# Float64 weights narrowed by a rounded integer low part from ScalarE and one integer add on GpSimd

## The chip, the cores and the metric

One core of one Trainium2 chip runs the whole program. The metric is the device time of one execution in microseconds (us); what is compared is the median over several executions. The engines are named as in the profile: PE is TensorE, DVE is VectorE, ACT is ScalarE, POOL is GpSimd and SP is SyncE, whose queue issues all the DMAs of this kernel.

## The reference

Attention with packed queries, then a gated feed-forward block, then a second feed-forward block, over 4608 tokens of width 512. The weight matrices arrive as float64 (the division by a square root promotes them), everything else as float32.

```
q, k, v: (8, 8, 576, 64)   p: (8, 8, 32, 64)   float32
p_packed = softmax_attention(p, k, v)
out      = softmax_attention(q, p_packed, p_packed)      -> x (4608, 512)
xn  = x / rms(x) * rms_g
g   = xn @ w_gate ;  val = xn @ w_val                    (512 x 1536, float64)
y   = (silu(g) * val) @ w_out                            (1536 x 512, float64)
h   = y @ w_in ;  a = max(h, 0) + alpha * min(h, 0)      (512 x 2048, float64)
out = a @ w_out2                                         (2048 x 512, float64)
```

## The kernel before

The tokens are cut into nine chunks of 512. Each chunk of the first feed-forward block runs 12 steps `f`: a matmul group into `ps_g` (gate), one into `ps_v` (value), `s = silu(g)` on ACT (L736), `s = s * v` on DVE (L742), a split of `s` into a high part `hh` (ACT, L68) and a low part `hl` (DVE, L71), and a matmul group into `ps_y`. Every product is three matmuls of high and low parts (L80 to L82). After all nine chunks, the second block runs over `y` read back from DRAM. Attention for the next chunk is cut into small steps (`k_steps`, `q_steps`) that are placed between the matmul groups at 34 places per chunk, by the function `attn`.

Before chunk 0 there is a prologue: it loads p, k, v and q, runs the attention of the first 512 tokens on banks of their own, with a few idle matmuls (`warmup`) between, and starts to narrow the weights. Each engine runs its instructions in the order in which the Python code emits them; nothing reorders them.

The narrowing is what the change touches. A weight unit is 128 x 512 float64 values, loaded as pairs of 32-bit words into a tile `w` (tag w64; `lo` and `hi` are its even and odd words, so each of them has a stride of 8 bytes). Units come in jobs of six: four of gate and value weights (`gv`, four DMAs each, L167) and two of `w_out` (`o`, one DMA each, L172); six jobs make the 36 units of the first block. `narrow` makes a float32 tile (`gv_raw` or `w_raw`) of a unit:

- L186, DVE: shift and mask of `hi` into the float32 tile.
- L191, ACT, on the units with `pool` set: `lo` scaled to a float.
- L193, DVE: sign and exponent bits of `hi` merged in. The tile is then the truncated float32.
- L197, DVE: the exponent alone, written over `hi`.
- L201, POOL (with `pool`): `lo` times the exponent, in place; or L204, DVE (without): scale and product in one instruction.
- L208, POOL: the tile plus that product, in float.

`narrow` is a generator: every `yield` ends a step. `conv(n)` runs `n` steps, two units alternating; `conv_to(m)` runs steps until `m` units are done. A unit of pool form has three steps, one of the other form four. The prologue asks for 30 steps; each of the 34 places of chunk 0 asks for three, and each `f` of chunk 0 forces with `conv_to` that the units it needs are done. A narrowed `gv` unit is also written to DRAM (L219, SP) so that later chunks can read it back (L562). The 32 units of the second block are narrowed by `conv_late` at the places that the table `LATE` selects in chunks 1 and on, and written to DRAM (L227).

The wide tiles come from a ring: nine slots for units 0 to 17, four (`NST`) for units 18 to 35. A load into a slot waits until the last instruction that reads the slot's old unit, which is the add on POOL, has ended. The loads, the writes of L219 and the loads of k, v and q (L122, L125, L137) all stand in one SP queue, in order: one that waits holds up all behind it.

Of the kernel before, what the change touches and what calls it, by code (L numbers as in the profile page):

```python
# [8 lines left out]
F32 = mybir.dt.float32  # L9
F32R = mybir.dt.float32r  # L10
I32 = mybir.dt.int32
U32 = mybir.dt.uint32
ACTF = mybir.ActivationFunctionType
ALU = mybir.AluOpType
# [4 lines left out]
def attention_moe_moe2_kernel(ctx, tc, q, k, v, p, w_gate, w_val, w_out, rms_g, w_in2, w_out2, alpha, out):  # L19
    nc = tc.nc  # L20
# [18 lines left out]
    scale = 1.0 / float(D) ** 0.5  # L39
# [2 lines left out]
    NST = 4  # L42
    SLOTS = dict(enumerate(["k"] * 10 + ["kk"] + ["k"] * 6 + ["a"]))
    SLOTS.update({20: "a", 21: "ba", 23: "a", 24: "a", 25: "a", 26: "b", 27: "b", 28: "a", 29: "b", 30: "b", 31: "b", 32: "b"})
    LATE = [int(i % 3 != 2) for i in range(34)]

    const = ctx.enter_context(tc.tile_pool(name="const", bufs=1))
    wa = ctx.enter_context(tc.tile_pool(name="wa", bufs=NF))
# [13 lines left out]
    def bank(tag):  # L62
        if tag in ("g", "v", "at", "wg"):
            return ps.tile([128, 512], F32, tag="m", name="ps_" + tag, bufs=4)
        return ps.tile([128, 512], F32, tag=tag, name="ps_" + tag)
# [18 lines left out]
    with tc.manual_schedule():  # L84
# [65 lines left out]
        raw, staged = {}, {}  # L150
# [8 lines left out]
        def load_wide(u, pool, bufs):  # L159
            t = pool.tile([128, 4, 128, 2], I32, tag="w64", name="w64", bufs=bufs)  # L160
            if u[0] == "gv":
                j, dc = divmod(u[1], 4)
                tf = t.rearrange("p c x w -> p (c x w)")
                for i, w in enumerate((w_gate, w_val)):
                    src = w.bitcast(I32).rearrange("(g c d) x -> c g d x", g=G, c=HG)[dc]
                    for g in range(G):
                        nc.sync.dma_start(  # L167
                            out=tf[g * D:(g + 1) * D, i * 512:(i + 1) * 512],
                            in_=src[g, :, j * 512:(j + 1) * 512],
                        )  # L170
            else:
                nc.sync.dma_start(out=t.rearrange("p c x w -> p c (x w)"), in_=src_of(u).bitcast(I32))  # L172
            return t

        def new_gv():
            return one.tile([128, 4, 128], F32, tag="gv", name="gv_raw", bufs=8)
# [2 lines left out]
            half = n * 2 // NU1  # L179
            staged[n] = load_wide(units[n], (sg, one)[half], (NSG, NST)[half])  # L180

        def narrow(t, w, pool):
            lo, hi = t[:, :, :, 0], t[:, :, :, 1]
            wi = w.bitcast(I32)
            r = lo.bitcast(F32)
            nc.vector.tensor_scalar(  # L186
                out=wi, in0=hi, scalar1=3, scalar2=0x3FFFFFF8,
                op0=ALU.logical_shift_left, op1=ALU.bitwise_and,
            )
            if pool:  # L190
                nc.scalar.activation(out=r, in_=lo.bitcast(U32), func=ACTF.Copy, scale=2.0 ** -52)  # L191
            yield
            nc.vector.scalar_tensor_tensor(  # L193
                out=wi, in0=hi, scalar=-0x40000000, in1=wi, op0=ALU.bitwise_and, op1=ALU.bitwise_or
            )
            yield
            nc.vector.tensor_scalar(  # L197
                out=hi, in0=wi, scalar1=-0x800000, scalar2=None, op0=ALU.bitwise_and
            )
            if pool:  # L200
                nc.gpsimd.tensor_tensor(out=r, in0=r, in1=hi.bitcast(F32), op=ALU.mult)  # L201
            else:
                yield
                nc.vector.scalar_tensor_tensor(  # L204
                    out=r, in0=lo.bitcast(U32), scalar=2.0 ** -52, in1=hi.bitcast(F32),
                    op0=ALU.mult, op1=ALU.mult,
                )
            nc.gpsimd.tensor_tensor(out=w, in0=w, in1=r, op=ALU.add)  # L208

        def conv_unit(n, pool):  # L210
            if n == NU1 // 2:
                sg_ctx.close()
                late_pools["wg2"] = ctx.enter_context(tc.tile_pool(name="wg2", bufs=NWG - NWG1, reuse_waits="tile"))
            u = units[n]
            w = new_gv() if u[0] == "gv" else wa.tile([128, 4, 128], F32, tag="w", name="w_raw")
            yield from narrow(staged.pop(n), w, pool)
            raw[u] = w
            if u[0] == "gv":
                nc.sync.dma_start(out=gv_dram[u[1]], in_=w.rearrange("p c x -> p (c x)"))  # L219
            yield  # L220

        def conv_late():
            ahead = [load_wide(u, one, NST) for u in units2[:2]]
            for i, u in enumerate(units2):
                w = one.tile([128, 4, 128], F32, tag="w32", name="w32", bufs=2)
                yield from narrow(ahead.pop(0), w, i % 2)
                nc.sync.dma_start(out=w_dram[i], in_=w)  # L227
                if i + 2 < len(units2):
                    ahead.append(load_wide(units2[i + 2], one, NST))
                yield  # L230
# [3 lines left out]
        def loads_to(n):  # L234
            while n_load[0] < min(n, NU1):
                m = n_load[0]
                old = m - (NSG, NST)[m * 2 // NU1]
                if old >= n_conv[0] and old >= 0 and old * 2 // NU1 == m * 2 // NU1:
                    break
                load_unit(m)  # L240
                n_load[0] += 1

        def conv_all():
            while n_conv[0] < NU1:
                n = n_conv[0]
                loads_to(NU1)
                while n // 6 > n_job[0] + 1:
                    yield
                live = [conv_unit(n, 1), conv_unit(n + 1, 1 if n % 3 else 0)]
                while live:  # L250
                    for g_ in list(live):
                        if next(g_, live) is live:
                            live.remove(g_)
                            n_conv[0] += 1
                            loads_to(NU1)
                        else:
                            yield
            while True:
                yield

        convs = conv_all()
        late = conv_late()

        def conv(n):
            for _ in range(n):
                next(convs, None)
# [337 lines left out]
        def warmup(n):  # L604
            for _ in range(n):
                nc.tensor.matmul(warm_bank[:, 0:128], lhsT=ident, rhs=ident, start=True, stop=True)

        def run(g_, n=1):
            for _ in range(n):
                next(g_, None)  # L610
# [13 lines left out]
        for n in range(14):  # L624
            run(gk)
            if n == 9:
                run(qa)
            if n in (6, 8, 10, 11, 12):
                conv(2)
        nc.sync.dma_start(out=alpha_sb, in_=alpha.rearrange("(f p) -> p f", p=128))  # L630
        for n, (g_, k_) in enumerate([(qa, 1), (qb, 1), (qa, 1), (qa, 1), (qb, 1), (qa, 2), (qb, 1), (qa, 1), (qb, 1), (qb, 3)]):
            conv(2)
            run(g_, k_)
            warmup(3)
        conv_to(4)
# [45 lines left out]
        for c in range(NCH):  # L681
# [10 lines left out]
            def attn():  # L692
                for g_ in SLOTS.get(slot[0], ""):
                    if g_ in gens:
                        run(gens[g_])
                slot[0] += 1
                if c == 0:
                    conv(3)
                elif not last and LATE[slot[0] - 1]:
                    next(late, None)  # L700

# [20 lines left out]
            for f in range(NF):  # L722
# [12 lines left out]
                s = ring.tile([128, T], F32, tag="s", name="s")  # L735
                nc.scalar.activation(out=s, in_=tg, func=ACTF.Silu)  # L736
                attn()
                if last and f == NF - 1:
                    both(("i2", 0))
                    both(("i2", 1))  # L740
                tv = blk_in(f, 256, "v")
                nc.vector.tensor_tensor(out=s, in0=s, in1=tv, op=ALU.mult)  # L742
                hs[f] = hsplit(s)
                attn()
                if f % 2:
                    if f < NF - 1:
# [5 lines left out]
                if f and f < NF - 1:  # L752
                    attn()
# [49 lines left out]
        for k_, (c, f) in enumerate(steps):  # L803
            if f == 0:
                ycur = ynext
            t = bank("g")
            wh, wl = in_s.pop(("i2", f))
            for d in range(KD):
# [3 lines left out]
                out=s, in0=t, scalar1=0.0, scalar2=alpha_sb[:, f:f + 1], op0=ALU.min, op1=ALU.mult  # L812
# [47 lines left out]
```

## Time and profile before

| | us |
|---|---|
| median of three runs | 1780.98 (1780.61 to 1782.32) |
| profiled execution, its own time | 1781.89 |
| its span | 1780.1 |
| busy in the span: PE, DVE, ACT, POOL | 1716.0, 1067.9, 776.4, 164.9 |
| prologue, up to the transposes of `x` for chunk 0 | 66.25 |
| chunk 0, from there to those for chunk 1 | 136.44 |
| chunk 1, likewise | 107.81 |

Stretches are cut where PE begins the transposes (L545) that make the `xh` and `xl` of a chunk: at 66.25, 202.69 and 310.50 us. A row of the waits view says which engine and line sat idle, for whose instruction, and for how long in total. In a row of the group view, the mean of one instruction counts from its start to its end, so an instruction that is held after it has started shows a long duration, not idle time. The granted clock of PE (PEclk) is a share of its full speed.

### The profile page before, as it was taken

The page shows a single profiled execution, that of the slowest core. Times are in us where ns is not written, and L with a number is a line of the kernel's source. Part 1 is how long each engine was busy: PE and PEld are TensorE (multiplying, and loading weights), DVE is VectorE, ACT ScalarE, POOL GpSimd, SP SyncE. Part 2 cuts the span into 40 slices and gives each one's busy share as a digit, 9 for nine tenths or more (in the row PEclk, how much of TensorE's full clock was granted, in tenths as well). Part 3 has the DMA queues.
Part 4 walks back from the last instruction along what each step waited for, and adds up shares of the span by engine and source line. Part 5 has one row for each costly group of instructions (what it writes and reads, how often), then busy time and mean ns, then how long its engine had stood idle before and what let it go on. Part 6 is the DMA issues. An engine that isn't in the chain of part 4 may idle for free.

```text
span 1780.1 us, 25459 instructions
## 1 busy us (share of the span) xinstructions
PE 1716.0 (96%) x9932; PEld 1395.2 (78%) x9932; DVE 1067.9 (60%) x1774; ACT 776.4 (44%) x1360; POOL 164.9 (9%) x142
## 2 busy tenths in 40 slices
PE   5778999999999999999999999999999999999999
PEld 4545778888888888888888888888888888888887
DVE  3888555655656665444344666666666666666665
ACT  2444455555555555554444333333333333333332
POOL 2565111011111111000000000000000000000000
PEclk7988999999999999999999999999999999999999
DMA  7857354555646463322142201010101010100000
GB/s 187 231 167 220 120 166 124 168 143 165 186 148 170 158 178 103 108 83 87 45 149 83 77 1 48 1 48 1 48 1 47 1 47 1 48 1 24 1 24 24
DMA packets 159064, 161.58 MB, mean 91 GB/s; under 512 B 88288, under 2 KB 102624, under 8 KB 158944
## 3 DMA queue, kind: packets, MB, share of 16 engines
q1 hardware_dynamic: 158944, 159.96, 29.7%
q8 instruction: 78, 1.28, 0.3%
q14 instruction: 42, 0.34, 0.1%
HBM read 126.36 MB, written 33.55 MB: 90 GB/s over the span
## 4 chain that ended last, share of the span: by engine, by line
PE 88%; DVE 4%; ACT 3%; DMA 2%; SPq 2%; issue 1%; POOL 0%; DVEq 0%; ACTq 0%
PE ps_y L80 13%; PE ps_y L82 12%; PE ps_y L81 12%; PE ps_g L82 11%; PE ps_g L80 11%; PE ps_g L81 11%; PE ps_v L80 3%; PE ps_v L81 3%; PE ps_v L82 3%; PE ps_wg L573 2%; PE ps_at L502 2%; PE ps_at L468 1%; SPq L167 1%; ACT L736 1%; PE ps_at L313 1%
## 5 line engine op out<-in xcount | busy, mean ns | idle before, releaser
L68 ACT ACTIVATE hh<-s2m 128x512 fp32r<-128x512 f32 x144 | 91.0, 632 | 493.7 <-DVE s2m L814 493.7
L71 DVE TENSOR_TENSOR in_l<-w_raw,in_h 128x512 fp32r<-128x512 f32 x306 | 211.0, 708 | 33.1 <-ACT in_h L68 28.8
L68 ACT ACTIVATE in_h<-w_raw 128x512 fp32r<-128x512 f32 x306 | 191.7, 627 | 80.9 <-PE ps_y L81 71.2
L81 PE MATMUL ps_g<-yl,in_h 128*128 128x512 f32 x576 | 226.6, 393 | 0.0
L80 PE MATMUL ps_g<-yh,in_h 128*128 128x512 f32 x576 | 226.3, 393 | 0.0
L82 PE MATMUL ps_y<-in_h,hl 128*128 128x512 f32 x576 | 226.0, 392 | 0.0
L82 PE MATMUL ps_g<-yh,in_l 128*128 128x512 f32 x576 | 225.8, 392 | 0.0
L80 PE MATMUL ps_y<-in_h,hh 128*128 128x512 f32 x576 | 225.2, 391 | 0.0
L81 PE MATMUL ps_y<-in_l,hh 128*128 128x512 f32 x576 | 223.9, 389 | 0.0
L811 DVE TENSOR_SCALAR s2m<-ps_g,alpha_sb 128x512 f32<-128x512 f32 x144 | 108.1, 750 | 162.9 <-PE ps_g L82 162.9
L80 PE MATMUL ps_y<-hh,in_h 128*128 128x512 f32 x432 | 180.4, 418 | 0.0
L81 PE MATMUL ps_y<-hl,in_h 128*128 128x512 f32 x432 | 169.4, 392 | 0.2 <-DVE hl L71 0.2
L82 PE MATMUL ps_y<-hh,in_l 128*128 128x512 f32 x432 | 169.5, 392 | 0.0
L71 DVE TENSOR_TENSOR hl<-s2m,hh 128x512 fp32r<-128x512 f32 x144 | 99.8, 693 | 109.3 <-ACT hh L68 109.3
L742 DVE TENSOR_TENSOR s<-s,ps_v 128x512 f32<-128x512 f32 x108 | 74.2, 687 | 128.2 <-PE ps_v L82 116.6
L68 ACT ACTIVATE hh<-s 128x512 fp32r<-128x512 f32 x108 | 68.2, 631 | 145.4 <-DVE s L742 144.9
L80 PE MATMUL ps_g<-xh,wgh 128*128 128x512 f32 (+7 forms) x384 | 126.5, 329 | 2.2 <-ACT xh L68 1.0
L80 PE MATMUL ps_v<-xh,wgh 128*128 128x512 f32 (+7 forms) x384 | 128.2, 334 | 0.0
L82 PEld LDWEIGHTS ps_g<-yh,in_l 128*128 128x128 f32 x576 | 108.1, 188 | 24.9
L81 PEld LDWEIGHTS ps_g<-yl,in_h 128*128 128x128 f32 x576 | 108.0, 188 | 25.0
L82 PE MATMUL ps_g<-xh,wgl 128*128 128x512 f32 (+7 forms) x384 | 122.9, 321 | 4.9 <-DVE wgl L71 4.8
L80 PEld LDWEIGHTS ps_g<-yh,in_h 128*128 128x128 f32 x576 | 108.1, 188 | 25.0
(151 smaller groups left out, 3095.7 us busy)
## 6 DMA issues: line engine op xcount, KB each, us to landing
gv_raw<-gv_dram SPq DMA_DIRECT2D x168, 256.0 KB, 4.2
w<-in_moe_w_out_dram SPq DMA_DIRECT2D x28, 512.0 KB, 4.0
kt<-in_k_dram SPq DMA_DIRECT2D x64, 144.0 KB, 3.5
vt<-in_v_dram SPq DMA_DIRECT2D x16, 576.0 KB, 5.6
y_dram<-stg SPq DMA_DIRECT2D x18, 512.0 KB, 2.7
y_raw<-y_dram SPq DMA_DIRECT2D x9, 1024.0 KB, 6.5
qt<-in_q_dram SPq DMA_DIRECT2D x64, 128.0 KB, 3.4
w<-in_moe_w_in_dram SPq DMA_DIRECT2D x16, 512.0 KB, 4.0
```

Of the source, the lines that this page charges most:

```text
L68: nc.scalar.activation(out=hi, in_=src, func=ACTF.Copy)
L71: nc.vector.tensor_tensor(out=lo, in0=src, in1=hi.bitcast(F32), op=ALU.subtract)
L80: nc.tensor.matmul(out=o, lhsT=lh, rhs=rh, start=first, stop=False)
L81: nc.tensor.matmul(out=o, lhsT=lh, rhs=rl, start=False, stop=False)
L82: nc.tensor.matmul(out=o, lhsT=ll, rhs=rh, start=False, stop=last)
L167: nc.sync.dma_start(out=tf[g * D:(g + 1) * D, i * 512:(i + 1) * 512], in_=src[g, :, j * 512:(j + 1) * 512],)
L313: nc.tensor.matmul(out=t[c * 64:(c + 1) * 64, 0:w], lhsT=pT[:, 2 * g + c, :], rhs=kT[g][:, c * S + hf * w:c * S + (hf + 1) * w], start=Tru ...
L468: nc.tensor.matmul(out=tv[off:off + n, k_, j], lhsT=qT[i][:, j, off:off + n], rhs=ppB[b % 2][:, j, :], start=True, stop=True,)
L502: nc.tensor.matmul(out=t[off:off + n, g * 256:(g + 1) * 256], lhsT=A2T[0][:, k_, g, off:off + n], rhs=ppbd[b % 2][:, :, g, :], start=True, ...
L573: nc.tensor.matmul(out=ts[g][h * NP:(h + 1) * NP, :], lhsT=ppG[b][g * D:(g + 1) * D, h, :], rhs=us[h][g * D:(g + 1) * D, :], start=True, s ...
L742: nc.vector.tensor_tensor(out=s, in0=s, in1=tv, op=ALU.mult)
L811: nc.vector.tensor_scalar(out=s, in0=t, scalar1=0.0, scalar2=alpha_sb[:, f:f + 1], op0=ALU.min, op1=ALU.mult)
```

## The change

L197, L201 and L204 go. ACT now runs on every unit, with another scale, and writes `lo` back as a rounded 32-bit integer in units of the float32's last place. POOL adds that integer to the bits of the truncated float32 in one integer add, where it had a float product and a float add. A unit has two steps instead of three or four, so the counts of steps change with it: in the prologue 2 of the 14 places of the first loop call `conv(2)` instead of 5, the second loop calls `conv(1)` instead of `conv(2)` (14 steps, seven units, instead of 30 steps), chunk 0 asks for two steps per place, and `LATE` selects every third place instead of two of three.

```diff
--- before.py
+++ after.py
@@ -42,7 +42,7 @@
     NST = 4
     SLOTS = dict(enumerate(["k"] * 10 + ["kk"] + ["k"] * 6 + ["a"]))
     SLOTS.update({20: "a", 21: "ba", 23: "a", 24: "a", 25: "a", 26: "b", 27: "b", 28: "a", 29: "b", 30: "b", 31: "b", 32: "b"})
-    LATE = [int(i % 3 != 2) for i in range(34)]
+    LATE = [int(i % 3 == 0) for i in range(34)]
 
     const = ctx.enter_context(tc.tile_pool(name="const", bufs=1))
     wa = ctx.enter_context(tc.tile_pool(name="wa", bufs=NF))
@@ -179,41 +179,27 @@
             half = n * 2 // NU1
             staged[n] = load_wide(units[n], (sg, one)[half], (NSG, NST)[half])
 
-        def narrow(t, w, pool):
+        def narrow(t, w):
             lo, hi = t[:, :, :, 0], t[:, :, :, 1]
             wi = w.bitcast(I32)
-            r = lo.bitcast(F32)
             nc.vector.tensor_scalar(
                 out=wi, in0=hi, scalar1=3, scalar2=0x3FFFFFF8,
                 op0=ALU.logical_shift_left, op1=ALU.bitwise_and,
             )
-            if pool:
-                nc.scalar.activation(out=r, in_=lo.bitcast(U32), func=ACTF.Copy, scale=2.0 ** -52)
+            nc.scalar.activation(out=lo, in_=lo.bitcast(U32), func=ACTF.Copy, scale=2.0 ** -29)
             yield
             nc.vector.scalar_tensor_tensor(
                 out=wi, in0=hi, scalar=-0x40000000, in1=wi, op0=ALU.bitwise_and, op1=ALU.bitwise_or
             )
-            yield
-            nc.vector.tensor_scalar(
-                out=hi, in0=wi, scalar1=-0x800000, scalar2=None, op0=ALU.bitwise_and
-            )
-            if pool:
-                nc.gpsimd.tensor_tensor(out=r, in0=r, in1=hi.bitcast(F32), op=ALU.mult)
-            else:
-                yield
-                nc.vector.scalar_tensor_tensor(
-                    out=r, in0=lo.bitcast(U32), scalar=2.0 ** -52, in1=hi.bitcast(F32),
-                    op0=ALU.mult, op1=ALU.mult,
-                )
-            nc.gpsimd.tensor_tensor(out=w, in0=w, in1=r, op=ALU.add)
-
-        def conv_unit(n, pool):
+            nc.gpsimd.tensor_tensor(out=wi, in0=wi, in1=lo, op=ALU.add)
+
+        def conv_unit(n):
             if n == NU1 // 2:
                 sg_ctx.close()
                 late_pools["wg2"] = ctx.enter_context(tc.tile_pool(name="wg2", bufs=NWG - NWG1, reuse_waits="tile"))
             u = units[n]
             w = new_gv() if u[0] == "gv" else wa.tile([128, 4, 128], F32, tag="w", name="w_raw")
-            yield from narrow(staged.pop(n), w, pool)
+            yield from narrow(staged.pop(n), w)
             raw[u] = w
             if u[0] == "gv":
                 nc.sync.dma_start(out=gv_dram[u[1]], in_=w.rearrange("p c x -> p (c x)"))
@@ -223,7 +209,7 @@
             ahead = [load_wide(u, one, NST) for u in units2[:2]]
             for i, u in enumerate(units2):
                 w = one.tile([128, 4, 128], F32, tag="w32", name="w32", bufs=2)
-                yield from narrow(ahead.pop(0), w, i % 2)
+                yield from narrow(ahead.pop(0), w)
                 nc.sync.dma_start(out=w_dram[i], in_=w)
                 if i + 2 < len(units2):
                     ahead.append(load_wide(units2[i + 2], one, NST))
@@ -246,7 +232,7 @@
                 loads_to(NU1)
                 while n // 6 > n_job[0] + 1:
                     yield
-                live = [conv_unit(n, 1), conv_unit(n + 1, 1 if n % 3 else 0)]
+                live = [conv_unit(n), conv_unit(n + 1)]
                 while live:
                     for g_ in list(live):
                         if next(g_, live) is live:
@@ -625,11 +611,11 @@
             run(gk)
             if n == 9:
                 run(qa)
-            if n in (6, 8, 10, 11, 12):
+            if n in (6, 10):
                 conv(2)
         nc.sync.dma_start(out=alpha_sb, in_=alpha.rearrange("(f p) -> p f", p=128))
         for n, (g_, k_) in enumerate([(qa, 1), (qb, 1), (qa, 1), (qa, 1), (qb, 1), (qa, 2), (qb, 1), (qa, 1), (qb, 1), (qb, 3)]):
-            conv(2)
+            conv(1)
             run(g_, k_)
             warmup(3)
         conv_to(4)
@@ -695,7 +681,7 @@
                         run(gens[g_])
                 slot[0] += 1
                 if c == 0:
-                    conv(3)
+                    conv(2)
                 elif not last and LATE[slot[0] - 1]:
                     next(late, None)
```

The first place is DVE in the prologue, at the second softmax of the first two query tiles. `s2_...` holds the row maxima and sums, `A2_...` the probabilities, `w64_...` a wide tile, `gv_raw_...` and `w_raw_...` the narrowed ones; the exponential runs on ACT between the subtraction (L475, in the new code L461) and the sum (L481, L467). Before:

```order
L474 TENSOR_REDUCE s2_324<-ps_y3_428 128x16
L475 TENSOR_TENSOR A2_323<-ps_y3_428,s2_324 128x512
L197 TENSOR_SCALAR w64_195<-gv_raw_409 128x512
L186 TENSOR_SCALAR w_raw_454<-w64_200 128x512
L186 TENSOR_SCALAR w_raw_482<-w64_202 128x512
L193 SCALAR_TENSOR_TENSOR w_raw_454<-w64_200,w_raw_454 128x512
L481 TENSOR_REDUCE s2_324<-A2_323 128x16
L482 TENSOR_SCALAR s2_324<-s2_324 128x16
L483 RECIPROCAL s2_324<-s2_324 128x16
L484 TENSOR_TENSOR A2_323<-A2_323,s2_324 128x512
```

And now:

```order
L460 TENSOR_REDUCE s2_323<-ps_y3_416 128x16
L461 TENSOR_TENSOR A2_322<-ps_y3_416,s2_323 128x512
L185 TENSOR_SCALAR gv_raw_431<-w64_195 128x512
L191 SCALAR_TENSOR_TENSOR gv_raw_413<-w64_190,gv_raw_413 128x512
L467 TENSOR_REDUCE s2_323<-A2_322 128x16
L468 TENSOR_SCALAR s2_323<-s2_323 128x16
L469 RECIPROCAL s2_323<-s2_323 128x16
L470 TENSOR_TENSOR A2_322<-A2_322,s2_323 128x512
```

Between the subtraction and the sum stood four narrowing instructions; now there are two, and the narrowing comes about two units later.

The second place is the SP queue in chunk 0, around the loads of units 24 and 25 (before `w64_1105` and `w64_1110`, now `w64_1019` and `w64_1024`); `kt_...` is a k tile of a later batch. Before:

```order
L172 DMA w64_1020<-in_moe_w_out_dram 128x1024
L219 DMA gv_dram_77<-gv_raw_1022 128x512
L219 DMA gv_dram_77<-gv_raw_1025 128x512
L122 DMA kt_1100<-in_k_dram 96x6x64 x4
L167 DMA w64_1105<-in_moe_w_gate_dram 64x512 x2
L167 DMA w64_1105<-in_moe_w_val_dram 64x512 x2
L167 DMA w64_1110<-in_moe_w_gate_dram 64x512 x2
L167 DMA w64_1110<-in_moe_w_val_dram 64x512 x2
```

And now:

```order
L172 DMA w64_945<-in_moe_w_out_dram 128x1024
L205 DMA gv_dram_77<-gv_raw_947 128x512
L205 DMA gv_dram_77<-gv_raw_989 128x512
L167 DMA w64_1019<-in_moe_w_gate_dram 64x512 x2
L167 DMA w64_1019<-in_moe_w_val_dram 64x512 x2
L167 DMA w64_1024<-in_moe_w_gate_dram 64x512 x2
L167 DMA w64_1024<-in_moe_w_val_dram 64x512 x2
L122 DMA kt_1073<-in_k_dram 96x6x64 x4
```

The loads of units 24 and 25 stood behind a load of k that waits for PE to give its buffer back; now they stand ahead of it, behind the two writes to DRAM that wait for POOL.

## Rows read from the trace of the kernel before

**Rows 1.** Stretches: length, PE, PEld, DVE, ACT, POOL busy (x), PEclk, DMA share, GB/s.

```profile
0.00:66.25 66.25, 41.67 (x337) 34.47 (x337) 34.48 (x67) 20.37 (x46) 21.23 (x26) 0.79 0.81 195
66.25:202.69 136.44, 107.38 (x617) 71.99 (x610) 108.73 (x172) 65.53 (x117) 69.21 (x55) 0.85 0.62 179
202.69:310.50 107.81, 107.45 (x765) 86.40 (x766) 58.39 (x116) 54.92 (x97) 13.59 (x11) 1.00 0.51 155
```

**Rows 2.** Same view: the stretch of the wide loads, and its two busiest 20 us.

```profile
52.40:179.00 126.60, 97.47 (x568) 65.73 (x567) 105.84 (x166) 58.88 (x108) 70.24 (x55) 0.84 0.73 207
60.00:80.00 20.00, 18.07 (x111) 12.54 (x109) 15.95 (x27) 10.79 (x21) 7.93 (x8) 0.91 0.92 237
80.00:100.00 20.00, 15.42 (x53) 9.47 (x52) 18.00 (x25) 9.88 (x20) 13.17 (x10) 0.74 0.88 246
```

**Rows 3.** Waits of PE in chunk 0: who, for whom, total us, times, longest.

```profile
PE ps_at L357 <- ACT E1T L75: 8.5, 1, 8.5
...
PE ps_at L313 <- DVE s L742: 3.9, 1, 3.9
```

**Rows 4.** Timeline of ACT in chunk 0: start, us, line, tiles [idle before <-releaser].

```profile
132.61 0.68 ACT L191 ACTIVATE w<-w 128x512 f32<-128x512 uint32 x1 [7.96 <-DMA w<-in_moe_w_val_dram]
```

**Rows 5.** Waits of the SP queue, then of DVE, in chunk 0; same columns.

```profile
SPq L219 <- POOL gv_raw L208: 39.2, 15, 9.7
...
DVE gv_raw L186 <- DMA w<-in_moe_w_val_dram: 7.8, 4, 4.0
```

**Rows 6.** DVE groups in chunk 0: line, tiles, xcount; busy us, mean ns; idle before.

```profile
L186 DVE TENSOR_SCALAR gv_raw<-w 128x512 int32<-128x512 int32 x16 | 14.0, 903 | 7.8 <-DMA w<-in_moe_w_val_dram 7.8
L193 DVE SCALAR_TENSOR_TENSOR gv_raw<-w,gv_raw 128x512 int32<-128x512 int32 x16 | 13.6, 869 | 0.0
L71 DVE TENSOR_TENSOR hl<-s,hh 128x512 fp32r<-128x512 f32 x11 | 11.7, 1059 | 7.7 <-ACT hh L68 7.7
L71 DVE TENSOR_TENSOR in_l<-w_raw,in_h 128x512 fp32r<-128x512 f32 x12 | 11.6, 963 | 0.3 <-ACT in_h L68 0.3
L186 DVE TENSOR_SCALAR w_raw<-w 128x512 int32<-128x512 int32 x10 | 10.6, 1083 | 1.6 <-DMA w<-in_moe_w_out_dram 1.6
...
L197 DVE TENSOR_SCALAR w<-gv_raw 128x512 int32<-128x512 int32 x18 | 6.8, 422 | 0.0
L193 DVE SCALAR_TENSOR_TENSOR w_raw<-w,w_raw 128x512 int32<-128x512 int32 x10 | 6.6, 679 | 0.0
L204 DVE SCALAR_TENSOR_TENSOR w<-w 128x512 f32<-128x512 uint32 x4 | 5.6, 1410 | 0.1
L197 DVE TENSOR_SCALAR w<-w_raw 128x512 int32<-128x512 int32 x10 | 3.8, 420 | 0.0
```

**Rows 7.** POOL groups in chunk 0, same columns.

```profile
L201 POOL TENSOR_TENSOR w<-w 128x512 f32<-128x512 f32 x24 | 27.9, 1164 | 48.1 <-DVE w L197 19.0 <-issue 10.6 <-ACT E L330 7.0
L208 POOL TENSOR_TENSOR gv_raw<-gv_raw,w 128x512 f32<-128x512 f32 x18 | 25.2, 1408 | 1.1
L208 POOL TENSOR_TENSOR w_raw<-w_raw,w 128x512 f32<-128x512 f32 x10 | 14.7, 1470 | 0.8
```

**Rows 8.** View of one line, two lines: xcount, ns min/median/max, first and last start.

```profile
L186 DVE TENSOR_SCALAR w<-w x32: 414/422/1411, 215.0 to 690.6; 128x512 int32<-128x512 int32 x32
...
L191 ACT ACTIVATE w<-w x46: 654/674/711, 19.2 to 690.3; 128x512 f32<-128x512 uint32 x46
```

**Rows 9.** Wait of PE in the prologue, columns as in rows 3.

```profile
PE ps_y L374 <- DVE ppbd L365: 2.6, 1, 2.6
```

**Rows 10.** Timeline of DVE in the prologue: start, us, line, tiles.

```profile
42.74 0.69 DVE L475 TENSOR_TENSOR A<-ps_y,s 128x512 f32<-128x512 f32 x1
...
46.90 0.68 DVE L481 TENSOR_REDUCE s<-A 128x16 f32<-128x512 f32 x1
...
52.74 0.69 DVE L475 TENSOR_TENSOR A<-ps_y,s 128x512 f32<-128x512 f32 x1
...
56.40 0.67 DVE L481 TENSOR_REDUCE s<-A 128x16 f32<-128x512 f32 x1
```

## The prediction

> **What bounds the kernel now.** I first cut the span into stretches and looked at PE, the engine that the page shows busy for 96% of it. From chunk 1 on there is nothing to win: in chunk 1 PE is busy 107.45 of 107.81 us at full clock, with DVE at 58.39 [rows 1]. The loss lies ahead of it. In chunk 0 PE is busy 107.38 of 136.44 us, at a mean granted clock of 0.85, and it issues fewer matmuls (617) than chunk 1 does (765) in 107.81 us. Chunk 0 could thus be done in about 107.8 x 617 / 765 = 87 us if PE waited for nothing. The prologue of 66.25 us has PE busy for 41.67.
>
> Chunk 0 is also where the weights are narrowed, and DVE is busy for 108.73 of its 136.44 us. What ends PE's waits there is DVE itself (L313 waits 3.9 us for L742) or ACT with a narrowing instruction ahead in its queue: the longest wait, 8.5 us for E1T, is the time in which ACT, and DVE with it, wait for the load of unit 24 (ACT sat idle 7.96 us before it) [rows 3, 4]. Two things therefore limit chunk 0 in turn: the order and load of DVE, and the arrival of wide tiles. The second hangs on the first: the SP queue stood 39.2 us in 15 waits for POOL's add before it could write a gv unit to DRAM, with the next loads queued behind, while DVE waited only 7.8 us for gv loads [rows 5].
>
> Then I compared durations. L186 has a median of 0.422 us over the late units, and means of 0.903 and 1.083 us in chunk 0; `hl` and `in_l` run 1.059 and 0.963 us where the same size in L193 takes 0.679 [rows 6, 8]. The long ones are those that run while POOL works. So each POOL instruction costs DVE time too.
>
> **The change, part by part.** The sum is made in the profiled execution (1781.89 us, span 1780.1), which lies 0.9 us above the median; savings are taken off the median, 1780.98.
>
> *Prologue.* Nine and a half units were started there, seven are now, each with fewer DVE instructions. Between the subtraction L475 and the sum L481 there is only an exponential on ACT to wait for, but 46.90 - (42.74 + 0.69) = 3.5 us pass in one case and 56.40 - (52.74 + 0.69) = 3.0 in the other [rows 10]. Now one L186 and one L193 stand there: 0.42 + 0.68 = 1.1 us. That gives back 2.4 and 1.9 us. PE's wait of 2.6 us for `ppbd` [rows 9] stood behind L197, L204 and L186; behind only two L193 I give back 2 of it. Together 6 us, less one or two collisions with POOL at the mean found below (0.5 us): 5 us. The bounds are 2 us (if narrowing just moves in front of something else) and 7.
>
> *DVE in chunk 0, work.* L197 goes: 6.8 + 3.8 = 10.6 us. L204 goes: 4 x 0.68 = 2.7 us at its undisturbed length. But since the prologue narrows less, two more L186 and four more L193 fall into chunk 0 (28 and 30 for 26 and 26 [rows 6]): 2 x 0.42 + 4 x 0.68 = 3.6 us. Net 9.7 us off DVE.
>
> *DVE in chunk 0, stretching by POOL.* Excess over the undisturbed length: L186 24.6 - 26 x 0.42 = 13.7; the sixteen L193 on gv tiles 13.6 - 10.9 = 2.7; `hl` 11.7 - 7.5 = 4.2; `in_l` 11.6 - 8.1 = 3.5; L204 5.6 - 2.7 = 2.9. That is 27.0 us over 52 POOL instructions [rows 6, 7], 0.52 each. POOL now has 30 in chunk 0: 15.6 us, so 11.4 us less. Bounds: nothing saved (each add costs twice as much because DVE now runs closer together) and 16 (if half the adds meet DVE in an instruction that doesn't mind).
>
> The Trainium skill, page "SBUF — State Buffer", section "SBUF: two separate sides", describes the mechanism: GpSimd and those VectorE instructions that use two ports or have two SBUF inputs take one pair of ports, exclusively and for a whole instruction. Here L186 at 0.42 us alone and 1.08 on average beside POOL agrees. If every add cost its full length, as that rule allows, the sum would lose its largest term; that is the second rival below.
>
> *The add on POOL.* No integer add stands in the trace. The nearest row is the float add L208 with the same tiles and strides, 1.41 to 1.47 us [rows 7]; the lower bound is the product L201 at 1.16, the upper one the pair that it replaces, 2.6. I take 1.43. The Trainium skill, page "GPSIMD Engine Reference", section "Engine selection", says that GpSimd adds 32-bit integers natively; it gives no time, and no run so far shows one.
>
> *ACT.* Six more units in the first block and 16 late ones at 0.674 us [rows 8], with another output type. ACT is busy 65.53 of 136.44 us in chunk 0 [rows 1]; cost nothing. Without that slack it would be 4 us for the six.
>
> *SP and the loads.* A write to DRAM now waits for one POOL instruction after L193 in place of L197 and two POOL instructions: up to 0.42 + 1.16 = 1.6 us sooner in each of 15 waits, 24 of the 39.2 us. The loads of units 24 and 25 now precede the load of k that waited for PE, so the 8.5 us wait of PE should shrink most. Then the transfers themselves limit. From 52.4 us, when the narrowed units begin to be written, to 179 us, when the last wide load has landed, 126.6 us at 207 GB/s make 26.2 MB. In the two best 20 us the rate was 237 and 246 GB/s [rows 2]; the same bytes at these rates take 110.6 and 106.5 us, 16 and 20 us less.
>
> *Late units.* 32 L197 and 16 L204 leave chunks 1 to 5, where DVE has slack; the conversions now end a chunk later, well ahead of chunk 8 that reads them. Nothing, within 2 us.
>
> *Sum.* DVE would allow 5 + 9.7 + 11.4 = 26 us, SP's waits 24 besides the prologue, the transfers 16 to 20. The last is the tightest, so it is the one that decides: 18 us. 1780.98 - 18 = 1763. Its own range is 1780.98 - 29 = 1752 (everything DVE gives, and the waits of PE at half clock with it) to 1771 (10 us: the prologue and half of the net work).
>
> **The rivals.** *Loads as late as before.* The second unit of each pair still has its L193 behind `in_l` and L319 in DVE's queue, one gv unit still takes four DMAs of SP's queue, and the ring still has four slots. If these set the pace, only the prologue and a few waits are won: some 6 us, 1775. For it speaks that DVE waits for loads already now [rows 5] and would wait more; against it, that the loads are held by POOL, which the change shortens.
>
> *POOL holds DVE in full.* When DVE is back to back, each add may hold it for its whole 1.43 us. 30 x 1.43 = 43 us replace the 27 measured, and DVE ends at 108.7 - 9.7 - 27 + 43 = 115, 6 us more than now; with 5 us from the prologue the time is 1782, no change. The 0.52 us of now, with POOL no less tightly behind DVE, speaks against it.
>
> *The integer add is slow.* This is the one that ends slower. A job of six units takes 136.44 / 6 = 22.7 us now; an add of more than 3.8 us makes POOL the bound of chunk 0. At 4.3 us (three times L208), six adds take 25.8 us, and chunk 0 grows by 6 x 3.1 = 18 us: 1799. Nothing in the trace is like it: the float forms take 1.16 to 1.47 us [rows 7].
>
> **How the numbers follow.** The forecast (1752 to 1771) gets 0.62, the late loads (1771 to 1777.4) 0.17, POOL's hold 0.12, the slow add 0.07, and 0.02 is left for another loss. A measurement of this kernel can tell about 0.2%, 3.6 us, from no change; so faster is 0.79, same 0.12, slower 0.09. The range of 1752 to 1777 holds the first two, eight in ten.
>
> **What would show it.** The transposes that open chunk 1 should stand at about 185 us instead of 202.69, those of chunk 0 at about 61 instead of 66.25, and chunk 1 should still take 107 to 108 us. DVE in chunk 0 should be busy for about 88 us, L186 shorter on average than 0.9 us. POOL's add should take 1.2 to 1.6 us. PE's wait for E1T should be under 4 us, its granted clock in chunk 0 over 0.9, and the DMA rate from 52 us on 230 to 246 GB/s. The prediction is wrong if chunk 0 keeps its length with DVE idle for loads (first rival), or with DVE still busy for over 105 us (second), or if POOL is busy through chunk 0 (third).

## The result and the profile after

The changed kernel takes 1758.38 us (median of four runs, 1757.34 to 1759.01) against 1780.8 for the kernel before, measured beside it (four runs, 1778.86 to 1782.32): a ratio of 0.9874, 95% interval 0.9857 to 0.9891, or 22.4 us less. The forecast was 18 less, 1763, with a range of 1752 to 1777. The profiled execution took 1759.01 us, its span 1757.2, which is 22.9 below the span before.

The three stretches, as in [rows 1], read from the windows of the kernel after (columns: start and end, length, busy time and instructions of PE, PEld, DVE, ACT and POOL, granted clock, DMA share, GB/s). Behind them stand two windows of 20 us and the stretch of the wide loads, as in [rows 2].

```profile
0.00:61.47 61.47, 41.55 (x337) 34.42 (x337) 22.01 (x51) 20.32 (x46) 11.85 (x18) 0.78 0.82 193
61.47:179.56 118.09, 102.38 (x617) 69.68 (x610) 85.39 (x146) 69.60 (x124) 43.62 (x33) 0.93 0.75 215
179.56:287.20 107.64, 107.08 (x765) 86.33 (x766) 54.08 (x104) 56.56 (x100) 7.90 (x7) 1.00 0.48 148
60.00:80.00 20.00, 16.06 (x96) 9.87 (x95) 15.28 (x23) 11.07 (x21) 9.28 (x7) 1.00 0.95 254
80.00:100.00 20.00, 17.79 (x87) 11.38 (x86) 17.27 (x29) 14.59 (x27) 9.77 (x8) 0.91 0.88 248
50.00:156.00 106.00, 88.07 (x537) 59.30 (x536) 78.56 (x132) 61.06 (x113) 43.52 (x32) 0.90 0.86 239
```

The prologue ends at 61.47 instead of 66.25 us (4.8 less), chunk 0 is 118.09 instead of 136.44 us long (18.3 less), and chunk 1 is 107.64, as before. So all of the gain is there by 179.56 us. Chunk 0 issues the same 617 matmuls. PE is busy 5.0 us less for them, at a mean granted clock of 0.93 instead of 0.85, and idle 13.3 us less (29.06 before, 15.71 now).

The waits of SP's queue and of DVE in chunk 0 after (engine and line, for whose instruction: us in total, times, longest), to be held against [rows 5]:

```profile
SPq L205 <- POOL gv_raw L194: 10.4, 7, 2.8
SPq L548 <- PE ps_wg L559: 9.0, 1, 9.0
...
DVE hl L71 <- ACT hh L68: 8.0, 11, 1.1
DVE w_raw L185 <- DMA w<-in_moe_w_out_dram: 7.7, 3, 4.8
```

The write to DRAM (L205, L219 before) now stands 10.4 us for POOL instead of 39.2. The wait for loads is no smaller for it: 7.7 us and 2.8 more for a gv load. PE's waits in chunk 0, against [rows 3], have no piece like the 8.5 us for E1T any more:

```profile
PE ps_at L442 <- ACT s L722: 3.3, 1, 3.3
PE ps_at L343 <- ACT E1T L75: 2.0, 1, 2.0
```

And the narrowing itself in chunk 0 by groups of DVE and POOL (busy us, mean ns of one, idle before), against [rows 6, 7]:

```profile
L191 DVE SCALAR_TENSOR_TENSOR gv_raw<-w,gv_raw 128x512 int32<-128x512 int32 x20 | 16.4, 830 | 0.0
L71 DVE TENSOR_TENSOR in_l<-w_raw,in_h 128x512 fp32r<-128x512 f32 x12 | 10.4, 868 | 2.1 <-ACT in_h L68 1.8
L185 DVE TENSOR_SCALAR gv_raw<-w 128x512 int32<-128x512 int32 x18 | 9.7, 546 | 2.8 <-DMA w<-in_moe_w_val_dram 2.8
L191 DVE SCALAR_TENSOR_TENSOR w_raw<-w,w_raw 128x512 int32<-128x512 int32 x10 | 8.8, 896 | 0.0
L71 DVE TENSOR_TENSOR hl<-s,hh 128x512 fp32r<-128x512 f32 x11 | 8.0, 730 | 8.0 <-ACT hh L68 8.0
L185 DVE TENSOR_SCALAR w_raw<-w 128x512 int32<-128x512 int32 x10 | 6.9, 700 | 7.8 <-DMA w<-in_moe_w_out_dram 7.7
...
L194 POOL TENSOR_TENSOR gv_raw<-gv_raw,w 128x512 int32<-128x512 int32 x20 | 28.0, 1401 | 37.2 <-DMA qt<-in_q_dram 7.8 <-DVE gv_raw L191 6.0 <-DMA w<-in_moe_w_val_dram 4.8
L194 POOL TENSOR_TENSOR w_raw<-w_raw,w 128x512 int32<-128x512 int32 x10 | 13.9, 1395 | 19.9 <-DVE st L322 10.1 <-DVE w_raw L191 7.4 <-DMA w<-in_moe_w_gate_dram 1.0
```

The integer add takes 1.40 us. L185 (L186 before) takes 0.55 and 0.70 us on average instead of 0.90 and 1.08. Over the undisturbed lengths L185 has 16.6 - 28 x 0.42 = 4.8 us too much, L191 25.2 - 30 x 0.68 = 4.8, `hl` 0.5 and `in_l` 2.2: 12.3 us over 30 adds, 0.41 each (0.52 per POOL instruction before).

### The profile page after: what moved, and what is told of

It reads as the page before. It is cut to its first block, busy times and chain, and to the rows that moved or that the text cites. A ratio compares the mean times of both kernels' runs of the same rounds, so it can differ in the third digit from the quotient of the medians.

```text
span 1757.2 us, 25350 instructions
## 1 busy us (share of the span) xinstructions
PE 1710.6 (97%) x9932; PEld 1392.7 (79%) x9932; DVE 1006.4 (57%) x1684; ACT 789.6 (45%) x1382; POOL 106.8 (6%) x96
## 4 chain that ended last, share of the span: by engine, by line
PE 88%; DMA 3%; ACT 3%; DVE 3%; SPq 1%; issue 1%; POOL 0%; ACTq 0%; DVEq 0%; POOLq 0%
PE ps_y L80 13%; PE ps_y L82 13%; PE ps_y L81 12%; PE ps_g L82 11%; PE ps_g L80 11%; PE ps_g L81 11%; PE ps_v L80 3%; PE ps_v L82 3%; PE ps_v L81 3%; PE ps_wg L559 2%; PE ps_at L488 2%; PE ps_at L454 2%; ACT L722 1%; DMA w<-in_moe_w_out_dram 1%; PE ps_at L299 1%
## 5 line engine op out<-in xcount | busy, mean ns | idle before, releaser
L82 PEld LDWEIGHTS ps_g<-yh,in_l 128*128 128x128 f32 x576 | 108.1, 188 | 24.9
L82 PEld LDWEIGHTS ps_y<-in_h,hl 128*128 128x128 f32 x576 | 108.1, 188 | 24.2 <-DVE hl L71 0.5
L81 PEld LDWEIGHTS ps_y<-in_l,hh 128*128 128x128 f32 x576 | 108.2, 188 | 23.7
```

The lines of the kernel that those rows point to most:

```text
L81: nc.tensor.matmul(out=o, lhsT=lh, rhs=rl, start=False, stop=False)
L82: nc.tensor.matmul(out=o, lhsT=ll, rhs=rh, start=False, stop=last)
```

## The experiments

Two theories stood against each other on why chunk 0 shortened by 18.3 us. By the prediction's own, the costs are bounds side by side, and the tightest one, the transfers, decides. By the other, they stand in a row: the time at which a unit's add ends sets when its write to DRAM can leave SP's in-order queue, and with it when the loads behind it start; every us of DVE or POOL in that row counts. Each kernel below changes the kernel after, except e1 and e7, which change the kernel before; times are medians, ratios are to the kernel before on the same chip.

**The pacing alone (e1).** The old narrowing with the new, thinner share of the prologue.

```diff
-            if n in (6, 8, 10, 11, 12):
-                conv(2)
+            if n in (6, 10):
+                conv(3)
...
-            conv(2)
+            conv(2 - n % 2)
```

> The kernel before, with the narrowing as it was, but with only as many units started in the prologue as the new kernel starts (seven instead of nine and a half). If the gain of the change comes from the pacing, this one has most of it: about 1762 us. If it comes from the work that is taken off VectorE and GpSimd (my theory), the prologue ends 3 to 5 us sooner, the units left out have to be narrowed in chunk 0, where VectorE is full, and the time is 1778 to 1786 us.

Measured: 1784.66 us, ratio 1.0028 (1.0019 to 1.0037). The prologue ended 6.8 us sooner, at 59.44, and chunk 0 took 146.60, 10.2 longer. Fewer units in the prologue are no gain in themselves.

**The units back in the prologue (e2).** Nine and a half units instead of seven.

```diff
-            if n in (6, 10):
+            if n in (6, 8, 10, 12):
...
-            conv(1)
+            conv(1 + n // 9)
```

> The new kernel, with nine and a half units started in the prologue as in the kernel before. If the pacing matters, it loses what the prologue won, 4 to 5 us: 1763 us. If transfers set the pace of chunk 0 (my theory), a prologue that ends later is made up for by units that are ready sooner, and the time stays within 2 us of 1758.

Measured: 1757.42 us, ratio 0.9868 (0.9852 to 0.9885), the same as the kernel after. Prologue and chunk 0 trade less than a microsecond (62.39 and 117.62), so fewer units are no gain with the cheaper narrowing either. e1 and e2 together say that the gain comes from the narrowing, not from its pacing.

**The mask back on DVE (e3), POOL's work doubled (e4), both (e5).** e3 puts L197's instruction back, one of DVE per unit, whose result nobody needs. e4 halves ACT's scale and lets POOL double the integer before it adds it, so POOL has two instructions per unit again. e5 does both, and comes near to the work of the kernel before in the structure of the kernel after: 60 POOL instructions and 30 masks in chunk 0 for its 52 and 28, but no product on DVE (L204).

```diff
+            nc.vector.tensor_scalar(
+                out=hi, in0=wi, scalar1=-0x800000, scalar2=None, op0=ALU.bitwise_and
+            )
```

> The new kernel with the removed mask on VectorE put back (68 instructions of 0.42 us, 30 of them in chunk 0, its result unused). If VectorE's load still sets the pace of chunk 0, it costs its 12 us there: 1770 us. If transfers now set it (my theory), most of the 12 us hide in the 33 us in which VectorE sits idle in chunk 0: 1759 to 1764 us.

```diff
-            nc.scalar.activation(out=lo, in_=lo.bitcast(U32), func=ACTF.Copy, scale=2.0 ** -29)
+            nc.scalar.activation(out=lo, in_=lo.bitcast(U32), func=ACTF.Copy, scale=2.0 ** -30)
...
+            nc.gpsimd.tensor_tensor(out=lo, in0=lo, in1=lo, op=ALU.add)
             nc.gpsimd.tensor_tensor(out=wi, in0=wi, in1=lo, op=ALU.add)
```

> The new kernel with a second instruction on GpSimd per unit (the integer low part is made half as large on ScalarE, so rounded one bit coarser, and doubled by an integer add in place), about 1.16 us each, 30 of them in chunk 0. If GpSimd's part of the path from a unit to its write and to the next load was what the change freed, this takes back 10 us or more: 1768 to 1772 us. If it was VectorE's own instructions, it costs VectorE only the stretching of about 0.4 us for each, 12 us of which idle time hides most: 1760 to 1764 us.

> The new kernel with both put back: the mask on VectorE and a second GpSimd instruction per unit (low part rounded one bit coarser). VectorE gets 12.6 us of work and about 12 us of stretching in chunk 0, which fill its 33 us of idle time. If the sum of VectorE's work and its stretching is the cause of the gain, most of the gain is gone: 1772 to 1780 us. If transfers alone decided, 1760 to 1765 us.

Chunk 0 of e3, e4 and e5 by windows, and in each SP's wait for POOL and DVE's waits for loads:

```profile
62.41:187.11 124.70, 104.72 (x616) 69.51 (x608) 99.25 (x176) 69.65 (x124) 43.43 (x33) 0.89 0.67 202
SPq L208 <- POOL gv_raw L197: 22.1, 12, 4.5
...
DVE w_raw L185 <- DMA w<-in_moe_w_out_dram: 3.3, 1, 3.3
...
DVE gv_raw L185 <- DMA w<-in_moe_w_val_dram: 0.9, 1, 0.9
```

```profile
61.30:190.87 129.57, 103.64 (x617) 69.31 (x609) 100.81 (x146) 69.73 (x124) 80.58 (x63) 0.91 0.64 192
SPq L206 <- POOL gv_raw L195: 27.6, 14, 4.7
...
DVE w_raw L185 <- DMA w<-in_moe_w_out_dram: 4.8, 1, 4.8
DVE gv_raw L185 <- DMA w<-in_moe_w_val_dram: 3.0, 2, 2.8
```

```profile
62.26:198.90 136.64, 108.45 (x616) 70.42 (x608) 116.42 (x176) 69.66 (x124) 81.16 (x63) 0.88 0.60 182
SPq L209 <- POOL gv_raw L198: 42.8, 16, 7.1
...
DVE gv_raw L185 <- DMA w<-in_moe_w_val_dram: 0.5, 1, 0.5
```

Measured: e3 1768.81 us, ratio 0.9934 (0.9919 to 0.9949), 10.4 above the kernel after; e4 1770.95, ratio 0.9947 (0.9932 to 0.9962), 12.6 above; e5 1783.14, ratio 1.0016 (1.0006 to 1.0025), 24.8 above, and 3 us beyond the range expected of it. The two costs add up (10.4 + 12.6 = 23.0, against 24.8 for both) and together undo the whole gain. Chunk 0 shows it best: it grows by 6.6 us in e3, by 11.5 in e4 and by 18.6 in e5, and the change had taken 18.3 off it. With a bound that decides alone, the first of the two would have been nearly free, which is what the theory behind the 18 us expected of e3. So the costs lie in a row. In e4, 60 POOL instructions cost DVE 26.7 us of stretching, 0.45 each, worked out as above. What stays open in e3: of the 11.4 us by which its span is longer, 3.8 lie behind chunk 0 (187.11 to 803.29 against 179.56 to 791.95 us), where the late units have the mask too.

Through which wait the costs add up is shown only in part. The later the add ends, the longer SP's write waits for it (10.4, 22.1, 27.6 and 42.8 us in the kernel after, e3, e4 and e5). The rate that falls with it (215, 202, 192, 182 GB/s) proves nothing, because much the same bytes, 24.9 to 25.4 MB, are spread over a longer chunk. And DVE doesn't wait longer for loads: 10.5 us in the kernel after, 4.2, 7.8 and 0.5 in the three. In e5 it is busy for 116.42 of 136.64 us, and late loads are not what holds it. A kernel whose writes to DRAM leave through another queue wasn't run; without it, the part of SP's queue stays argued.

**The same DVE work in another place (e12).** One mask-like DVE instruction on an idle tile at each of the 34 places of chunk 0, ahead of the narrowing steps but not within a unit.

```diff
                 if c == 0:
+                    nc.vector.tensor_scalar(out=x, in0=x, scalar1=-0x800000, scalar2=None, op0=ALU.bitwise_and)
                     conv(2)
```

> The new kernel with one additional VectorE instruction at each of the 34 places of chunk 0, of the kind and size of the removed mask, on a tile that nobody else uses: as much work as the masks, but outside the path of a unit. If VectorE's time in order counts, whoever uses it, chunk 0 grows as with the masks (6.6 us): 1763 to 1767 us. If it counts only as a part of each unit's path from load to write, 1757 to 1761 us.

```profile
60.43:181.04 120.61, 102.53 (x617) 69.42 (x609) 96.94 (x179) 69.61 (x124) 44.83 (x32) 0.92 0.72 211
SPq L207 <- POOL gv_raw L196: 15.0, 9, 3.3
```

Measured: 1761.21 us, ratio 0.9895 (0.988 to 0.991). DVE is busy 96.94 us, nearly e3's 99.25, but chunk 0 grows by 2.5 us, not by 6.6. Eight of the 34 instructions run behind the merge of the last unit; but the 24 that start before 155 us take 14.9 us, as the masks of e3 do before 160 us (15.4), so the comparison holds. DVE's load in itself is the smaller part; what the mask cost was mostly its place between a unit's merge and its add.

**More bytes (e6 on after, e7 on before).** Three more loads of 256 KB per job in the same queue, into a tile that nobody reads.

```diff
             staged[n] = load_wide(units[n], (sg, one)[half], (NSG, NST)[half])
+            if n % 6 in (1, 3, 5):
+                x = one.tile([128, 512], I32, tag="x", name="x")
+                nc.sync.dma_start(out=x, in_=w_out[n // 6 * 128:n // 6 * 128 + 128, 0:256].bitcast(I32))
```

> The new kernel with 18 additional loads of 256 KB from the weights into a tile that nobody reads, three for each job of six units; 13 or 14 of them, 3.5 MB, fall into the stretch of the wide loads. If that stretch is bound by transfers (239 GB/s over 106 us), they cost 3.5 MB at that rate, 14 us: 1770 to 1774 us. If VectorE or the order of the queue binds it, they cost only 18 issues: 1758 to 1762 us.

> The kernel before with the same 18 additional loads. Its stretch runs at 207 GB/s; at 239 GB/s its 126.6 us have room for 4 MB. If it was bound by VectorE and the waits for GpSimd (my theory), the 3.5 MB cost much less than in the new kernel: 1781 to 1787 us. If it was bound by transfers all along, as much as there: 1793 to 1797 us.

Chunk 0 of e6, its waits, and then chunk 0 of e7:

```profile
61.39:189.69 128.30, 102.67 (x616) 70.85 (x608) 85.82 (x146) 70.22 (x124) 43.00 (x32) 0.88 0.78 232
SPq L208 <- POOL gv_raw L197: 4.7, 6, 1.6
...
SPq L183 <- DMA x<-in_moe_w_out_dram: 3.2, 2, 2.6
...
DVE w_raw L188 <- DMA w<-in_moe_w_out_dram: 14.7, 5, 7.7
```

```profile
68.23:206.14 137.91, 105.65 (x617) 71.37 (x609) 109.13 (x170) 65.49 (x117) 69.08 (x54) 0.86 0.69 205
```

Measured: e6 1765.79 us, ratio 0.9912 (0.9893 to 0.993), 7.4 above the kernel after, with chunk 0 10.2 longer. e7 1784.21, ratio 1.0018 (1.0009 to 1.0028), 3.8 above the kernel before, with chunk 0 1.5 longer and the prologue 2.0. The kernel before was not bound by its transfers: 205 x 137.91 - 179 x 136.44 = 3.8 MB more moved in nearly the same time. The kernel after is, in part: 232 x 128.30 - 215 x 118.09 = 4.4 MB more take 18 us at its 239 GB/s, and 10.2 of them appear, in the profile of the slowest of e6's four executions. Not all of that need be bytes, since the added loads share one tile, and SP stood 3.2 us until it was free for the next (L183). The result lies between the two expectations; how the limits of transfers and of the row through the add divide it isn't shown.

**Slots of the ring: five (e9) and three (e10).** e9 takes one slot from the first ring and one buffer of `y_raw` for it.

```diff
-    NSG = 9
-    NST = 4
+    NSG = 8
+    NST = 5
...
-            t = p2.tile([128, KD, T], F32, tag="y", name="y_raw", bufs=2)
+            t = p2.tile([128, KD, T], F32, tag="y", name="y_raw", bufs=1)
```

> The new kernel with five slots instead of four in the ring of wide tiles for units 18 to 35 (paid with one slot less for units 0 to 17, and one y buffer instead of two in the second block). If the pace of chunk 0 is the loop through a slot (load, VectorE, GpSimd, write, next load), so that every part of it counts in series, a fifth slot gives back several us: 1750 to 1755 us. If it is VectorE's order or the transfers alone, the loads come sooner but nothing ends sooner: 1756 to 1760 us.

e10 sets `NST = 3` and nothing else.

> The new kernel with three slots instead of four. If the loop through a slot sets the pace, the second half of chunk 0 (some 60 us) becomes a third longer: 1770 to 1780 us. If it is VectorE or transfers, little: 1758 to 1763 us.

Chunk 0 of e9 with SP's wait for POOL, and then of e10 with its waits:

```profile
60.52:177.38 116.86, 103.22 (x616) 69.25 (x609) 85.72 (x146) 69.36 (x124) 43.01 (x33) 0.91 0.75 220
...
SPq L205 <- POOL gv_raw L194: 4.1, 4, 1.5
```

```profile
61.21:201.77 140.56, 109.55 (x616) 73.44 (x608) 86.35 (x146) 69.89 (x124) 43.18 (x33) 0.85 0.62 183
SPq L205 <- POOL gv_raw L194: 25.5, 10, 4.7
DVE gv_raw L185 <- DMA w<-in_moe_w_val_dram: 18.0, 5, 5.1
DVE w_raw L185 <- DMA w<-in_moe_w_out_dram: 12.3, 3, 6.7
```

Measured: e9 1757.35 us, ratio 0.9873 (0.9858 to 0.9888), no different from the kernel after, though SP now waits only 4.1 us for POOL instead of 10.4. e10 1802.44, ratio 1.013 (1.0115 to 1.0145), slower than the kernel before and worse than expected; of the 44 us above the kernel after, 22 lie in chunk 0 and nearly all the rest behind it, in chunks 2 to 6 (3.1 to 4.8 us each), where the late units use the same ring. Four slots are just enough, as far as e9 can show it, which pays for the fifth elsewhere. e10 is also the picture of the first rival: chunk 0 long, DVE idle for loads (30.3 us), POOL's work unchanged. And it warns against reading SP's wait for POOL as time lost: e10 has 25.5 us of it with 140.56 us of chunk 0, e4 27.6 with 129.57.

**The narrowing later in the prologue (e8), and with five slots (e11).**

```diff
-            if n in (6, 10):
+            if n in (10, 12):
                 conv(2)
```

> The new kernel with the first two units of the prologue narrowed later (behind places 10 and 12 instead of 6 and 10), so that VectorE doesn't wait 7.8 us for a load ahead of the maxima that TensorE needs (a wait of 6.3 us for the exponential). If the prologue's chain sets the end of chunk 0, 4 to 6 us are won: 1753 us. If the transfers do (my theory), the prologue ends sooner but chunk 0 takes longer by as much: 1757 to 1759 us.

> Five slots, and the first two units narrowed later as in e8_conv_later. If what the two give adds up: 1746 to 1753 us. If the prologue's 5 us are lost to the transfers once the ring is no longer the limit: 1753 to 1757 us.

Measured: e8 1755.66 us, ratio 0.9858 (0.9842 to 0.9875). Its prologue ends at 56.52, 4.95 us sooner than after's, and its chunk 0 takes 117.67, so the lead stays; of it 2.7 us show in the median and 4.9 in the span (its profiled execution is the fastest of four, that of the kernel after the slowest). I had expected it to be given back. e11, which joins e8 and e9, has the lowest median of all, 1754.85, ratio 0.9864 (0.9848 to 0.988), with chunk 0 in 115.40 us. The intervals of both overlap that of the kernel after, so these runs don't tell them apart from it.

## Why the prediction held, and where its sum was off

*Prologue.* 5 us predicted, 4.8 measured, but not by all the pieces named. The rows of DVE in the prologue after (start, us, engine, line) answer to [rows 10]:

```profile
40.05 0.69 DVE L461 TENSOR_TENSOR A<-ps_y,s 128x512 f32<-128x512 f32 x1
...
41.60 0.68 DVE L467 TENSOR_REDUCE s<-A 128x16 f32<-128x512 f32 x1
42.31 0.83 DVE L468 TENSOR_SCALAR s<-s 128x16 f32<-128x16 f32 x1
...
48.10 0.69 DVE L461 TENSOR_TENSOR A<-ps_y,s 128x512 f32<-128x512 f32 x1
...
51.26 0.17 DVE L496 TENSOR_SCALAR s<-s 128x2 f32<-128x2 f32 x1 [2.14 <-ACT ps_y L493]
51.34 0.69 DVE L191 SCALAR_TENSOR_TENSOR w_raw<-w,w_raw 128x512 int32<-128x512 int32 x1
51.94 0.68 DVE L467 TENSOR_REDUCE s<-A 128x16 f32<-128x512 f32 x1
52.66 1.21 DVE L468 TENSOR_SCALAR s<-s 128x16 f32<-128x16 f32 x1
```

The first gap between subtraction (L461) and sum (L467) fell from 3.5 to 0.9 us, as worked out. The second stayed at 3.15 (3.0 before). A statistic (L496, before L510) stands ahead of this sum in DVE's queue in both kernels; now it waits 2.14 us for ACT, where before it found its input ready:

```profile
55.39 0.15 DVE L510 TENSOR_SCALAR s<-s 128x2 f32<-128x2 f32 x1
```

So for this second gap the prediction was wrong that only an exponential lies between the two. The wait for `ppbd` fell from 2.6 to 0.5 us, as predicted. These two pieces, 2.6 and 2.1 us, are about the 4.8.

*DVE's work and stretching.* 88 us of busy time predicted, 85.4 measured; 0.41 us per add instead of 0.52. The Trainium skill, page "SBUF — State Buffer", section "SBUF: two separate sides", has GpSimd hold the shared pair of ports for a whole instruction; L468 agrees: it takes 0.175 us in the median, and 1.21 in the row above, beside an add that began just before it. It ended at 53.87, the add at 53.83:

```profile
52.56 1.27 POOL L194 TENSOR_TENSOR w_raw<-w_raw,w 128x512 int32<-128x512 int32 x1
```

But most DVE instructions meet no such hold. Of the 28 L185 in chunk 0, 22 take 0.41 to 0.43 us and four 1.50 to 1.53; before, ten of the 26 L186 took 0.41 to 0.43 and the other sixteen 0.74 to 1.55. On average an add costs DVE 0.41 us and not its 1.40, so the second rival, which put 43 us there, is out.

*The add on POOL.* 1.43 us taken, 1.40 measured. The third rival needed over 3.8.

*SP and the loads.* The wait for POOL fell by 28.8 us; I had 24. The first rival is out: the loads came earlier, the last wide one landing at 155 us instead of 179. The sign given for it, 230 to 246 GB/s over the stretch, was met with 239, against 207 before.

*ACT and the late units.* Costs of nothing, and nothing is seen: chunk 1 takes 107.64 us, and all of the difference of the spans, 22.9, is there when it begins (23.1). Two more signs were met: PE's longest wait for E1T is 2.0 us (under 4 was forecast), and the granted clock in chunk 0 is 0.93 (over 0.9).

*The sum.* This is the step that failed in size. "The last is the tightest, so it is the one that decides: 18 us" treats the terms as bounds side by side, with the transfers starting at 52.4 us whatever the prologue does. By 179.56 us 23.1 us had been won, where I had written 185, because the prologue's 4.8 come on top of chunk 0's 18.3; the prediction's own signs, 61 and 185 us, left only 12.4 us to chunk 0. The loads themselves run from 50 to 156 us where they took from 52.4 to 179, so the transfers shrank by about the 20 us at the upper end of the estimate and started 2 us sooner. What failed is the rule for adding up. e3, e4 and e5 lengthen chunk 0 by 6.6, 11.5 and 18.6 us: two costs that add, which a single deciding bound doesn't allow. That the forecast came near all the same was partly luck: the three terms, 26, 24 and 16 to 20 us, lay so close together that none of them would have missed the measured 22.4 by much. What was missing is a sum along a unit's path, of DVE's work ahead of the add and of the add itself; these runs show that the two add, but not what each costs per unit.

What is left open is how the 118 us of chunk 0 divide now between transfers and order. e6 says that bytes count at about half their price; a kernel with fewer bytes wasn't run. Open too is how much of the path runs through SP's queue (the write, the next load) and how much through DVE's own order.

## What to carry to other kernels

Where loads and writes share one in-order DMA queue, a write that waits for compute holds up every load behind it. And an instruction between a tile's last input and its write can cost far more than the same instruction a step away (6.6 against 2.5 us here for about the same DVE time). Bounds may be compared by their smallest only if they really run side by side; where one's end is the other's start, their savings add, and putting each removed cost back alone and then both together tells which it is.

## What the runs showed of the hardware that I had not expected

The integer add on GpSimd takes as long as the float add on the same tiles, 1.40 against 1.41 to 1.47 us, and ACT's conversion to a rounded integer as long as to a float (0.67 us). A DVE instruction on 16 elements per partition that takes 0.175 us in the median ran 0.83 and 1.21 us beside POOL's add; the other 16 of its kind, none of them beside a POOL instruction, were not stretched. So small instructions are held too, not only wide ones.
